# A fused attention and Fourier-mixing kernel: the third channel table's sines behind batch 0's last relu, absolute values by a sign mask, sign changes on three engines, batch 2's relay copies ahead

## Chip, cores and metric

The kernel runs on one core of one Trainium2 chip. The metric is the device time of one execution in microseconds (us); lower is better. The core has five engines with queues of their own: TensorE (PE, with its weight loads shown as PEld), VectorE (DVE), ScalarE (ACT), GpSimd (POOL) and SyncE (SP, which issues DMAs here).

## What is computed

Inputs are q, k and v of shape 8 x 12 x 448 x 64 (batch, heads, positions, head width) and two weights of 768 x 3072 and 3072 x 768, all float32.

```python
scores = q @ k.T / sqrt(64)
attn   = maximum(scores, 0) ** 2 / 448
x      = (attn @ v), heads side by side            # 8 x 448 x 768
u      = x + real(fft(fft(x, axis=positions), axis=channels))
un     = (u - mean(u)) / sqrt(var(u) + 1e-6)       # over the 768 channels
out    = u + maximum(un @ w_ch1, 0) @ w_ch2
```

## The kernel before

**Stages.** For each batch b the kernel brings q and k into transposed form (`turning`), makes scores for two heads and a quarter of the keys at a time (24 steps in a batch, line 857), takes the relu on ScalarE (line 870, PSUM to SBUF) and the square on VectorE (line 887), and multiplies by v (lines 842 and 785). After four steps one block m of 128 channels (m = 0 to 5) is complete: it is scaled and copied out of PSUM as the tile `xT` (lines 594 and 596 for batch 0, 612 later), and its two halves along the positions are added and subtracted (`fold`; `first_fold`, line 671, for batch 0).

**Mixing.** The Fourier transforms are matmuls with cosine and sine tables: `chan[0..2]` over the channels, `seq` over the positions. Blocks m = 3 to 5 use the same channel tables as m - 3, one half with its sign changed: `chan_neg[m - 3]`. For batch 0 the channel matmuls are `first_channels` (line 1307): for two row blocks i and six blocks m; two wide products for each i and m below 3, four half as wide for m from 3 on. Their sum is copied out (`pc`, line 1351), multiplied by `seq` and its negative `nseq`, normalised and transposed (`first_tail`), and only then can the first FFN matmul run (line 1793). From then on FFN matmuls of earlier tokens (lines 1793, 1821, 1848, 1933) are mixed with the attention and mixing of the later batches.

**The tables.** `build_dft` makes them on the chip. `turns` takes three VectorE operations: the product of column and row number, rounded to an integer (line 311); the difference, a fraction of a turn f (line 313); and the absolute value g as max(-f, f) (line 315). `sine` then takes two ScalarE sines from f and g (line 320). `channel_table(0)` comes first, `others()` makes tables 1 and 2. `negative()` makes `nseq` and the three `chan_neg` on VectorE (lines 357 and 361). `root_table()` (line 367) is a ScalarE square root of one column, which has the table of square roots loaded before the norm needs it.

**Transposes.** Batches 0 and 1 are transposed on TensorE (line 545), copied out on VectorE or ScalarE (line 552). From batch 2 on, VectorE copies q and k into the relay tile `qkr` (line 509), and DMAs transpose that into `qkT` (line 521). `turn_rest` starts this as one stream for batches 1 to 7.

**The order of the work.** Nothing of the order is left to the hardware's luck: a planner (`Streams.run`) draws it up when the kernel is built. Each piece of work is a stream that asks with `need(engine, us, dependencies, buffers)`. The planner always issues the request that can start earliest by its own clocks; between equals the lower rank goes first. A stream is added with two ranks, the first for TensorE, the second for all other engines:

```python
key = (ok is not None and not ok(), max(t), s[1][eng != "PE"])
```

So the estimated durations and the ranks decide the order on every engine, and a changed estimate anywhere can change the order of all that follows. On the chip, each engine then goes through its own queue strictly in that order, and waits at a semaphore where a result is not there yet. `warming` (line 2011, rank 9) fills TensorE's gaps with matmuls on zeros until batch 0's channel matmuls are done; it adds into the first of the three double banks `psS`, which then becomes the sum of the channel matmuls for i = 0. Squares have rank 0.2, copies of xT rank 0, folds of batch 0 rank 0.3, the table operations of `others` 0.15, `negative` 0.35, `turning` for batch 0 0.15, and `turn_rest` 2.

GpSimd's queue also issues the loads of q, k, v (line 413) and of the weights (lines 443 and 454); each of them waits until the load eight before it has landed.

Of the kernel before, what the change touches and what calls it, by code (L numbers as in the profile page):

```python
# [166 lines left out]
def kernel(  # L167
# [9 lines left out]
    nc = tc.nc  # L177
# [125 lines left out]
    def build_dft():  # L303
        row, col, col2 = drow, dcol, dcol2

        def turns(f, g, cols, rows, n, i):

            d = dve(n) + 0.04
            yield need("DVE", d, [indices_ready])
            r = work.tile([128, 2 * KH], mybir.dt.int32, name="dftr", tag=f"pc{TC[i][0]}", bufs=1)  # L310
            nc.vector.tensor_scalar(r[:, :n], cols, rows, None, op0=ALU.mult)
            yield need("DVE", d)
            nc.vector.scalar_tensor_tensor(f, cols, rows, r[:, :n], op0=ALU.mult, op1=ALU.subtract)
            e = yield need("DVE", d)
            nc.vector.scalar_tensor_tensor(g, f, -1.0, f, op0=ALU.mult, op1=ALU.max)
            return e

        def sine(dst, y, n, e, sign=1, bias=zero_t):
            e = yield need("ACT", act(n), [e + LATENCY["DVE"]])
            nc.scalar.activation(dst, y, AF.Sin, bias=bias, scale=sign * 2.0 * math.pi)  # L320
            dft_ready.t = e + LATENCY["ACT"]
# [13 lines left out]
        def channel_table(m):  # L335
            y = early_hid if m == 2 else work.tile([128, 4 * KH], FP32, name="dfty", tag=("u1A", "u1B")[m], bufs=1)
            e = yield from turns(y[:, 2 * KH:4 * KH], y[:, 0:2 * KH], col2, row[:, 4 + m:5 + m], 2 * KH, m % 2)
            yield from sine(chan[m][:, 0, :], y[:, 0:2 * KH], 2 * KH, e, -1, halfpi)
            yield from sine(chan[m][:, 1, :], y[:, 2 * KH:4 * KH], 2 * KH, e)
            chan_made[m].t = dft_ready.t  # L340
# [10 lines left out]

    chan_made, dft_all = [Cell() for _ in range(3)], Cell()

    def negative():

        e = yield need("DVE", 0.35, [seq_ready])
        nc.vector.tensor_scalar(nseq, seq[:, 1], -1.0, None, op0=ALU.mult)
        nseq_ready.t = e + LATENCY["DVE"]
        for m in range(3):
            e = yield need("DVE", 0.27, [chan_made[m]])  # L360
            nc.vector.tensor_scalar(chan_neg[:, m], chan[m][:, :, KH:], -1.0, None, op0=ALU.mult)
            chan_ready[m].t = e + LATENCY["DVE"]

    def root_table():

        yield need("ACT", 1.5, [dft_all, last_relu])
        nc.scalar.activation(drow[:, 7:8], zero_t, AF.Sqrt, bias=eps_t)
# [128 lines left out]

    def turning(bs):

        for b in bs:
            for g in range(NG):  # L500
                if b < 2:
# [68 lines left out]
    def fold(b, m, F, av, give, av_end):  # L570
# [58 lines left out]
        if b == 0:  # L629
# [662 lines left out]

    first_pps, first_chan = [None, None], [Cell(), Cell()]

    def first_channels(i, ms):

        n0, n1 = TC[i]
        for m in ms:
# [4 lines left out]
            for t in range(2):  # L1303
                parts = [(0, 2 * KH, chan[m][:, t, :])] if m < 3 else \
                    [(0, KH, chan[m - 3][:, t, 0:KH]), (KH, 2 * KH, chan_neg[:, m - 3, t, :])]
                for c0, c1, tab in parts:
                    nc.tensor.matmul(first_pps[i][:n1 - n0, t, c0:c1], lhsT=first_folds[m][:, t, n0:n1], rhs=tab,  # L1307
                                     start=(i == 1 and m == 0), stop=(m == MC - 1 and c1 == 2 * KH))
        if m < MC - 1:
            sch.add(first_channels(i, [MC - 1]), (0, 0))  # L1310
        else:
# [704 lines left out]
    with tc.manual_schedule():  # L2016
# [18 lines left out]
        sch.add(root_table(), (0, 0.4))  # L2035
        sch.add(negative(), (0, 0.35))
        for slot in range(6):
# [33 lines left out]
```

## Time and profile before

| what | value |
|---|---|
| median of three runs | 578.0 us (577.87 to 578.24) |
| the profiled execution | 577.99 us |
| its span in the trace | 576.0 us |
| granted TensorE clock | 1.00 |
| busy: PE, DVE, ACT, POOL | 565.0, 446.9, 336.9, 134.0 us |
| DMA, bytes moved | 81.84 MB |
| DVE, ACT busy from 17.5 to 30.4 us | 12.83 and 12.90 of 12.90 us |

Rows of the profile name the engine, the line of the kernel, the operation, and tiles as out<-in with their shapes. A busy share is an average over stages with different limits. TensorE's matmuls are pipelined, so that the lengths of neighbours overlap. Idle time is shown in square brackets with what ended it.

### The profile page before, as it was taken

How to read it: one execution, taken by the hardware profiler on the slowest of the kernel's cores; microseconds unless marked ns; L12 is line 12 of the kernel's file. 1: busy time of each engine (PE TensorE's matmuls, PEld its weight loads, DVE VectorE, ACT ScalarE, POOL GpSimd, SP SyncE). 2: the span in 40 equal slices, each digit the busy share in tenths (PEclk: the TensorE clock that was granted, in tenths of full speed). 3: DMA queues.
4: the chain of work that ended last, by engine and by line, in shares of the span. 5: the costliest groups of instructions: out<-in, count | busy, mean ns of one | idle time of the engine just before them, and what ended most of it. 6: DMA issues, size and time to landing. Idle time of an engine off the chain costs nothing.

```text
span 576.0 us, 11341 instructions
## 1 busy us (share of the span) xinstructions
PE 565.0 (98%) x4339; PEld 358.5 (62%) x4344; DVE 446.9 (78%) x1030; ACT 336.9 (59%) x538; POOL 134.0 (23%) x187
## 2 busy tenths in 40 slices
PE   8999999999999999999999999999999999999997
PEld 6466556544465546556757567568567786868864
DVE  6988775986688877997798879978978994267872
ACT  5977772977745676667559658856573160406400
POOL 8527102410134113321333116112220230000000
PEclk9999999999999999999999999999999999999999
DMA  9999999656938985799769977996654342223012
GB/s 125 206 211 249 202 219 181 174 109 78 202 78 223 175 140 119 161 167 193 140 136 197 201 126 161 177 173 113 141 107 94 109 142 85 66 73 93 2 41 97
DMA packets 133505, 81.84 MB, mean 142 GB/s; under 512 B 77516, under 2 KB 128716, under 8 KB 133452
## 3 DMA queue, kind: packets, MB, share of 16 engines
q0 software_dynamic: 40320, 33.63, 37.2%
q1 hardware_dynamic: 93132, 47.50, 36.6%
q8 instruction: 34, 0.56, 0.4%
q14 instruction: 19, 0.16, 0.1%
HBM read 62.91 MB, written 26.25 MB: 155 GB/s over the span
## 4 chain that ended last, share of the span: by engine, by line
PE 87%; DVE 9%; ACT 3%; issue 1%; DVEq 0%; ACTq 0%
PE psF L1793 31%; PE psF L1933 21%; PE psS L857 6%; PE psF L785 5%; PE psF L1821 4%; PE psS L1933 4%; PE psS L1635 3%; PE psF L1848 3%; PE psS L1332 2%; DVE sq L887 2%; ACT sq L870 1%; PE psS L785 1%; PE psS L2011 1%; PE psF L1635 1%; PE psS L932 1%; PE psS L1307 1%
## 5 line engine op out<-in xcount | busy, mean ns | idle before, releaser
L1793 PE MATMUL psF<-unT,w 128*128 128x256 bf16 (+2 forms) x1435 | 197.6, 294 | 1.3 <-ACT hT L1780 0.7
L870 ACT ACTIVATE sq<-psS 112x896 bf16<-112x896 f32 x192 | 165.2, 930 | 39.6 <-PE psS L857 39.2
L1793 PEld LDWEIGHTS <-w 128*128 128x128 bf16 x1440 | 137.5, 98 | 58.7 <-issue 12.9
L887 DVE TENSOR_TENSOR sq<-sq 112x896 bf16<-112x896 bf16 x163 | 98.4, 620 | 15.9 <-ACT sq L870 14.9
L1780 ACT ACTIVATE hT<-psF 128x512 bf16<-128x512 f32 (+3 forms) x144 | 71.7, 513 | 66.5 <-PE psF L1793 65.3
L1933 PEld LDWEIGHTS <-hT 128*128 128x128 bf16 x720 | 69.0, 98 | 50.3 <-issue 5.9
L1933 PE MATMUL psF<-w,hT 128*128 128x384 bf16 x378 | 67.1, 326 | 0.7 <-DVE xT L612 0.7
L1515 DVE TENSOR_TENSOR o<-psF,o 128x384 f32<-128x384 f32 x80 | 44.2, 553 | 25.2 <-PE psF L1933 20.8
L857 PE MATMUL psS<-qkT 64*128 64x448 bf16 (+1 forms) x384 | 52.8, 358 | 2.5 <-ACT sq L870 1.9
L413 POOL DMA_DIRECT2D vn<-in_v_dram x24 | 17.5, 730 | 105.4 <-PE psS L857 86.0
L1176 POOL TENSOR_TENSOR u<-tp,xn 112x385 f32<-112x385 f32 (+2 forms) x14 | 13.6, 974 | 109.0 <-DVE tp L1158 81.8
L857 PEld LDWEIGHTS <-qkT 64*128 64x128 bf16 (+1 forms) x384 | 17.3, 101 | 31.1 <-issue 24.1
L612 DVE TENSOR_SCALAR xT<-psF 128x224 bf16<-128x224 f32 x54 | 18.5, 383 | 21.8 <-PE psF L785 21.7
L785 PE MATMUL psF<-sq,vn 112*64 112x448 bf16 x264 | 31.3, 358 | 0.9 <-DVE hT L1778 0.9
L1204 ACT ACTIVATE un<-u,nmr,rstd 113x768 bf16<-113x768 f32 (+2 forms) x23 | 23.0, 1022 | 14.9 <-DVE nmr L1191 14.6
L413 POOL DMA_DIRECT2D qn<-in_q_dram x21 | 15.2, 724 | 62.7 <-DVE qkr L509 53.0
L1933 PE MATMUL psF<-wsum,hT 128*128 128x384 bf16 x162 | 28.8, 326 | 0.0
L1185 DVE BATCH_NORM_STATS2 stats<-u 112x6 f32<-112x384 f32 (+2 forms) x56 | 28.8, 540 | 0.0
L785 PEld LDWEIGHTS <-vn 112*64 112x64 bf16 x336 | 15.8, 109 | 19.6 <-issue 13.4
L884 ACT ACTIVATE sq<-sq 112x896 bf16<-112x896 bf16 x29 | 27.3, 950 | 0.5
L1821 PE MATMUL psF<-w,hT 128*128 128x384 bf16 x144 | 24.9, 326 | 0.0
L1848 PE MATMUL psF<-w,hT 128*128 128x384 bf16 x144 | 24.4, 326 | 0.0
(228 smaller groups left out, 783.2 us busy)
## 6 DMA issues: line engine op xcount, KB each, us to landing
out_dram<-o SPq DMA_DIRECT2D x56, 192.0 KB, 2.3
vn<-in_v_dram POOLq DMA_DIRECT2D x24, 224.0 KB, 5.0
qn<-in_q_dram POOLq DMA_DIRECT2D x21, 224.0 KB, 4.5
kn<-in_k_dram POOLq DMA_DIRECT2D x21, 224.0 KB, 7.3
w<-in_moe_w_ch_dram POOLq DMA_DIRECT2D x12, 384.0 KB, 13.2
w<-in_moe_w_ch_dram POOLq DMA_DIRECT2D x4, 1152.0 KB, 15.5
utop<-u SPq DMA_DIRECT2D x12, 336.0 KB, 3.8
o<-utop SPq DMA_DIRECT2D x16, 192.0 KB, 4.2
```

Of the source, the lines that this page charges most:

```text
L413: nc.gpsimd.dma_start(out=t, in_=src[b, hs].rearrange("h (p j) d -> p h (j d)", j=4))
L785: nc.tensor.matmul(av[h * Dh:(h + 1) * Dh, 0:S], lhsT=vn[:, c, h0 + h, :], rhs=sq[:, h, :], start=(c == 0), stop=(c == 3))
L857: nc.tensor.matmul(sc[:wide, h, 0:S].rearrange("k (c q) -> k c q", c=4), lhsT=flat[ps, k0:k0 + wide], rhs=qT[ps, m % 2], start=True, stop= ...
L870: nc.scalar.activation(r, sc[:R, :, 0:S], AF.Relu)
L887: nc.vector.tensor_tensor(r, r, r, op=ALU.mult)
L1185: nc.vector.bn_stats(stats[:n, hf, :], u[:n, hf * (D // 2):(hf + 1) * (D // 2)])
L1515: nc.vector.tensor_tensor(o, pc[:, 0:DH], o, op=ALU.add)
L1780: nc.scalar.activation(hs, ps, AF.Relu)
L1793: nc.tensor.matmul(ph[:, i * N:(i + 1) * N], lhsT=w1_sb[m][hf][:, (jj + i) * 128:(jj + i + 1) * 128], rhs=unT[:, m, 0:N], start=(m == 0), ...
L1821: nc.tensor.matmul(pc[:, 0:DH], lhsT=block(j, c), rhs=w2(j, hf), start=(j == 0), stop=(j == JC - 1))
L1848: nc.tensor.matmul(pc[:, 0:DH], lhsT=block(2 * i + k, c), rhs=weights[i], start=(start and i == 0), stop=(i == KP - 1), skip_group_check=True)
L1933: nc.tensor.matmul(pc[:, 0:DH], lhsT=lhs[i], rhs=rhs[i], start=(start and i == 0), stop=(i == KP - 1), skip_group_check=True)
```

## The change

1. In `turns` the absolute value is taken by clearing the sign bit: one VectorE operation with a constant on the 32-bit pattern. The planner's estimates for the first and third operation are lowered.
2. The two sines of channel table 2 get batch 0's last relu as a further dependency, so that they stand behind it in ScalarE's order.
3. The sign change of table 0 stays on VectorE, that of table 1 goes to GpSimd, that of table 2 to ScalarE. `root_table` also waits for the last. The rank of `negative` on these engines goes from 0.35 to 0.15.
4. The folds of batch 0 go from rank 0.3 to 0.2, level with the squares.
5. `first_channels` no longer goes through m = 0 to 4 in one stream: m = 0 comes first, then 1 to 4 are streams of their own in any order, and m = 5 follows when these are done.
6. `turn_rest` starts batch 1, then batch 2's group 0, then batch 2's groups 1 and 2 with rank 0.15 in place of 2, then batches 3 to 7.

```diff
         def turns(f, g, cols, rows, n, i):
             d = dve(n) + 0.04
-            yield need("DVE", d, [indices_ready])
+            yield need("DVE", d - 0.14, [indices_ready])
...
-            e = yield need("DVE", d)
-            nc.vector.scalar_tensor_tensor(g, f, -1.0, f, op0=ALU.mult, op1=ALU.max)
+            e = yield need("DVE", dve2(n))
+            nc.vector.tensor_scalar(g.bitcast(mybir.dt.int32), f.bitcast(mybir.dt.int32), 0x7FFFFFFF, None, op0=ALU.bitwise_and)
...
-        def sine(dst, y, n, e, sign=1, bias=zero_t):
-            e = yield need("ACT", act(n), [e + LATENCY["DVE"]])
+        def sine(dst, y, n, e, sign=1, bias=zero_t, deps=()):
+            e = yield need("ACT", act(n), [e + LATENCY["DVE"], *deps])
...
-            yield from sine(chan[m][:, 0, :], y[:, 0:2 * KH], 2 * KH, e, -1, halfpi)
-            yield from sine(chan[m][:, 1, :], y[:, 2 * KH:4 * KH], 2 * KH, e)
+            deps = [last_relu] if m == 2 else []
+            yield from sine(chan[m][:, 0, :], y[:, 0:2 * KH], 2 * KH, e, -1, halfpi, deps)
+            yield from sine(chan[m][:, 1, :], y[:, 2 * KH:4 * KH], 2 * KH, e, deps=deps)
...
         for m in range(3):
-            e = yield need("DVE", 0.27, [chan_made[m]])
-            nc.vector.tensor_scalar(chan_neg[:, m], chan[m][:, :, KH:], -1.0, None, op0=ALU.mult)
-            chan_ready[m].t = e + LATENCY["DVE"]
+            en = ("DVE", "POOL", "ACT")[m]
+            e = yield need(en, {"DVE": 0.27, "POOL": 0.7, "ACT": act(2 * KH)}[en], [chan_made[m]])
+            if en == "ACT":
+                nc.scalar.activation(chan_neg[:, m], chan[m][:, :, KH:], AF.Copy, scale=-1.0)
+                negated.t = e
+            else:
+                (nc.gpsimd if en == "POOL" else nc.vector).tensor_scalar(chan_neg[:, m], chan[m][:, :, KH:], -1.0, None,
+                                                                         op0=ALU.mult)
+            chan_ready[m].t = e + LATENCY[en]
 
     def root_table():
-        yield need("ACT", 1.5, [dft_all, last_relu])
+        yield need("ACT", 1.5, [dft_all, last_relu, negated])
...
     def turn_rest():
         yield need("SP", 0.0, [c for g in turned_at[0] for c in g])
-        sch.add(turning(range(1, B)), (2, 2))
+        sch.add(turning([1], range(NG)), (2, 2))
+        yield need("SP", 0.0, [*turned_at[1][2]])
+        sch.add(turning([2], [0]), (2, 2))
+        yield need("SP", 0.0, [*turned_at[2][0]])
+        sch.add(turning([2], [1, 2]), (2, 0.15))
+        yield need("SP", 0.0, [*turned_at[2][2]])
+        sch.add(turning(range(3, B), range(NG)), (2, 2))
...
-            sch.add(first_fold(m, x, f, gone.t + LATENCY["DVE"]), (0.3, 0.3))
+            sch.add(first_fold(m, x, f, gone.t + LATENCY["DVE"]), (0.3, 0.2))
...
     def first_channels(i, ms):
...
-        if m < MC - 1:
-            sch.add(first_channels(i, [MC - 1]), (0, 0))
+        if m == 0:
+            for x in range(1, MC - 1):
+                sch.add(first_channels(i, [x]), (5, 5))
+        elif m < MC - 1:
+            channels_made[i] += 1
+            if channels_made[i] == MC - 2:
+                sch.add(first_channels(i, [MC - 1]), (0, 0))
...
-            sch.add(first_channels(i, range(MC - 1)), (5, 5))
+            sch.add(first_channels(i, [0]), (5, 5))
...
-        sch.add(negative(), (0, 0.35))
+        sch.add(negative(), (0, 0.15))
```

More of the change, by code (lines that the diff above doesn't have):

```diff
@@ L350, in build_dft @@
         sch.add(others(), (0, 0.15))
-    chan_made, dft_all = [Cell() for _ in range(3)], Cell()
+    chan_made, dft_all, negated = [Cell() for _ in range(3)], Cell(), Cell()
     def negative():
@@ L495, with turning @@
     turned_at = [[[Cell() for _ in range(2)] for _ in range(NG)] for _ in range(B)]
-    def turning(bs):
+    def turning(bs, gs=range(NG)):
         for b in bs:
-            for g in range(NG):
+            for g in gs:
                 if b < 2:
@@ L1291, in second_turned @@
         un_left.t = group_ready[1].t = e
-    first_pps, first_chan = [None, None], [Cell(), Cell()]
+    first_pps, first_chan, channels_made = [None, None], [Cell(), Cell()], [0, 0]
     def first_channels(i, ms):
```

## The prediction

> **What bounds the kernel now.** I read the page's totals first, to see which engine could move the whole.
>
> ```profile
> span 576.0 us, 11341 instructions
> PE 565.0 (98%) x4339; PEld 358.5 (62%) x4344; DVE 446.9 (78%) x1030; ACT 336.9 (59%) x538; POOL 134.0 (23%) x187
> ```
>
> TensorE is busy 565.0 of 576.0 us, but that total counts filler matmuls (line 2011) that only keep the engine running while batch 0 is prepared. So I cut the span into stages with the busy-by-window view. Columns: window, its length, then busy us (and instructions) of PE, PE weight load, DVE, ACT, POOL, then granted clock, DMA share, GB/s.
>
> ```profile
> 8.00:17.50 9.50, 8.46 (x122) 5.43 (x120) 6.95 (x16) 8.89 (x13) 8.69 (x33) 1.00 1.36 178
> 17.50:30.40 12.90, 11.97 (x101) 5.87 (x100) 12.83 (x26) 12.90 (x20) 6.36 (x12) 1.00 1.18 210
> 30.40:37.20 6.80, 6.39 (x52) 3.98 (x50) 5.39 (x21) 4.69 (x8) 2.30 (x4) 1.00 1.08 211
> 37.20:48.30 11.10, 10.94 (x126) 8.53 (x127) 8.79 (x25) 7.57 (x18) 4.06 (x4) 1.00 1.16 224
> 48.30:64.00 15.70, 14.05 (x156) 7.79 (x155) 12.61 (x24) 12.37 (x17) 8.21 (x10) 1.00 1.19 232
> 64.00:130.00 66.00, 65.93 (x445) 36.14 (x443) 50.10 (x119) 43.55 (x65) 13.79 (x18) 1.00 0.95 173
> ```
>
> From 64 us on TensorE leaves 0.07 us unused in 66: there real FFN matmuls fill it, so work shifted on another engine is worth nothing unless a TensorE gap opens or closes. Before that, the opposite holds. From 17.5 to 30.4 us VectorE (12.83) and ScalarE (12.90) are both full, and no FFN matmul can run until batch 0 is through its attention, mixing and norm. A microsecond saved there moves the start of the FFN work, hence the end, by a microsecond. Then I read the chain in order of time over that stretch (start, length, what).
>
> ```profile
> 7.91 0.44 PE psS L2011 x6
> 8.35 0.53 PE psF L545 x16
> 8.91 0.91 ACT qkT L552
> 12.25 0.51 ACT chan L320
> 17.49 0.62 DVE qkT L552
> 20.20 0.56 DVE early L315
> 20.76 2.68 DVE sq L887 x5
> 34.41 2.79 PE psS L1307 x28
> 37.20 0.51 PE psF L545 x16
> ```
>
> From 8.91 the chain is on ScalarE, from 17.49 on VectorE (the third table's absolute value at 20.20 among the squares), and it ends in 28 channel matmuls in one block, 34.41 to 37.20. After that comes batch 0's mixing and norm, in which the diff changes nothing.
>
> **The change, part by part.** The durations of the VectorE forms in the first 37 us (groups by line with shapes apart; busy us, mean ns):
>
> ```profile
> L311 DVE TENSOR_SCALAR dftr<-dcol,drow 128x386 int32<-128x386 f32 x3 | 1.4, 477 | 0.0
> L313 DVE SCALAR_TENSOR_TENSOR dfty<-dcol,drow,dftr 128x386 f32<-128x386 f32 x2 | 1.2, 620 | 0.1
> L315 DVE SCALAR_TENSOR_TENSOR dfty<-dfty 128x386 f32<-128x386 f32 x2 | 1.1, 552 | 0.0
> L361 DVE TENSOR_SCALAR channeg<-chan 128x386 bf16<-128x386 bf16 x3 | 0.8, 290 | 0.0
> ```
>
> And the end of the stretch, in the timeline (start, length, engine, instruction):
>
> ```profile
> 32.06 1.16 ACT L870 ACTIVATE sq<-psS 112x896 bf16<-112x896 f32 x1
> 33.24 1.28 ACT L367 ACT_TABLE_LOAD   x1
> 34.53 0.29 ACT L367 ACTIVATE drow<-zero_t,eps_t 128x1 f32<-128x1 f32 x1
> 33.25 0.62 DVE L887 TENSOR_TENSOR sq<-sq 112x896 bf16<-112x896 bf16 x1
> 35.57 0.45 DVE L671 TENSOR_TENSOR fold<-xT 128x225 bf16<-128x225 bf16 x2
> 36.37 0.25 PE L1307 MATMUL psS<-chan,fold 128*128 128x193 bf16 x1
> 36.95 0.24 PE L1307 MATMUL psS<-channeg,fold 128*97 128x193 bf16 x1
> 36.90 1.05 ACT L1351 CAST pc<-psS 128x386 bf16<-128x386 f32 x2 [2.08 <-PE psS L1307]
> ```
>
> *Third table's sines behind the last relu.* Two sines at a net 0.51 us each (row at 12.25) leave the full ScalarE stretch: 1.02 us. The last relu, which now ends at 32.06 + 1.16 = 33.22, could end at 32.2. By itself this moves nothing, since VectorE is as full: it leaves VectorE alone as the limit. Behind the last relu then stand two sines (1.02) and the third sign change, taken at a sine's net 0.51 for the same 386 elements, then the table load 1.28 and the root 0.29: 32.2 + 3.1 = 35.3. The next ScalarE job, the pc copy, waits for the matmuls and stands idle 2.08 us today, so 35.3 is in time for anything later than that. The channel matmuls of m = 2 and 5 get their table at about 33.2 and 33.9, also ahead of the last fold. Cost nothing; if the relus do not come forward, 36.3 is still ahead of 36.90.
>
> A rule that speaks against this part is in the Trainium skill, "ScalarE: Activation LUTs", section "What ACT_TABLE_LOAD costs": beside a load of 1283 ns it counts a drain of about 1380 ns for every change of set. By that the queue would end at 36.7, half a microsecond behind the copy's new time and the sum below smaller by 0.5. The rows at 33.24 and 34.53 show the root starting 1.29 us after the load starts, so no drain behind the load, and the load starts 0.02 us after the last relu's end.
>
> *Absolute value by a mask.* Removed: 0.55 us each (386 elements). The new form is a one-input VectorE operation with a constant. Its nearest row is L311, 0.48 mean, which also carries a column scalar; line 313 against 315 prices that at 0.62 - 0.55 = 0.07. So 0.41, a bound of 0.55 if it is no faster, and 0.34 if the short instances count: I take 0.34, saving 0.21, because L311's mean holds one long first instance. Only the third table's is on the saturated chain; the first two lie before 17.49.
>
> *Sign changes on GpSimd and ACT.* Two times 0.25 (L361's three sum to 0.8 with one stretched) leave VectorE: 0.50. The first stays, only earlier. With the mask, VectorE's work between 17.49 and the last fold's end (35.57 + 0.45 = 36.02) drops by 0.21 + 0.50 = 0.71.
>
> *Channel matmuls one by one, folds level with squares, the first sign change ahead.* No work is added. Today the folds wait behind every square, so the matmuls pile up into the 28-block, and those of m = 5 start at 36.37 although the last fold ends at 36.02. If only these eight remain then, they start at 36.08 and end 36.37 - 36.08 = 0.29 us sooner. The price is that folds now delay squares: of VectorE's 0.71 up to all can come back as idle time if nothing is left for it between the last square and the last xT copy (33.25 + 0.62 to the fold: the values matmul and the copy lie between). Bound 0 to 0.7, taken 0, because a fold of m = 4 is still to be done there.
>
> *Start.* The second half of group 0's transposes (L545 x16) is planned only once the first half's copy has a place on VectorE, and 0.44 us of filler stands in front (row at 7.91). Two cheaper absolute values of the sequence tables let the plan place that copy sooner. Bounds 0 and 0.44; I take half, 0.2. ScalarE is full behind it, so it passes on.
>
> *GpSimd operation.* One row of GpSimd's queue there, then rows with both engines at SBUF, and one beside work from PSUM:
>
> ```profile
> 24.31 0.53 POOL L443 DMA_DIRECT2D w<-in_moe_w_ch_dram  x1 [1.33 <-DMA w<-in_moe_w_ch_dram]
> 101.00 1.26 POOL L1176 TENSOR_TENSOR u<-tp,xn 112x385 f32<-112x385 f32 x1
> 102.22 1.15 POOL L1178 TENSOR_TENSOR u<-qs,xn 112x383 f32<-112x383 f32 x1
> 101.41 1.27 DVE L1178 TENSOR_TENSOR u<-tp,xn 128x383 f32<-128x383 f32 x1
> 106.04 0.55 DVE L1178 TENSOR_TENSOR u<-tp,xn 112x383 f32<-112x383 f32 x1
> 41.55 0.98 POOL L1005 TENSOR_SCALAR un<-u,rstd,nmr 128x768 bf16<-128x768 f32 x1 [5.23 <-DVE nmr L976]
> ```
>
> GpSimd stands idle 1.33 us before a weight load, until an older load has landed; the new operation can take that place, and the loads queued behind it start later by less than its own length, with no reader of them before the FFN. Its real price is VectorE's. The VectorE addition takes 1.27 beside two GpSimd operations and 0.55 alone: 0.72 lost for 2.41 us of GpSimd, 0.3 per us. The new operation has half the elements of the one at 41.55 (0.98), so about 0.75 us: 0.22 lost. Ends 0 and 0.72. The Trainium skill, "SBUF — State Buffer", section "Who interferes with whom", says that a VectorE instruction with two SBUF inputs and a GpSimd one that reads SBUF exclude each other: whichever starts second is blocked fully. A square beside the operation would then lose up to the whole 0.75 and the sum would shrink by 0.5; the rows at 101 us agree that VectorE is held, by 0.72.
>
> *Batch 2's relay copies first.* Same four copies, earlier among VectorE's work between 95 and 113 us. What matters is what waits behind them:
>
> ```profile
> 98.29 0.43 DVE L509 COPY qkr<-kn 112x1024 bf16<-112x1024 bf16 x1 [2.19 <-DMA qkT<-qkr]
> 240.95 1.91 DVE qkr L509 x2
> 243.51 2.77 PE L1933 MATMUL psF<-w,hT 128*128 128x384 bf16 x16 [0.66 <-DVE xT L612]
> 359.78 0.95 PE L785 MATMUL psF<-sq,vn 112*64 112x448 bf16 x8 [0.93 <-DVE hT L1778]
> ```
>
> A relay copy can stand at the head of VectorE's queue until its buffer is free of the transpose before it: 2.19 us at 98.29, and the batch's mixing work queued behind it waited too. TensorE had FFN matmuls then (0.07 us unused from 64 to 130), so neither the wait nor its absence costs anything there. The rows at 240.95 and 243.51 show where it does cost: two relay copies of a later batch stand in front of an xT copy, and TensorE waits 0.66. The new streams give the whole order after 48 us a new draw. Such waits, 0.66 and 0.93, can close or open; TensorE's unused time from 48.3 to 64 is 15.70 - 14.05 = 1.65. Together 3.2 us are there to be had, and nothing in the rows limits what can open. I take a third of the 0.66, so -0.2, because one of its two causes, the relay stream, is rebuilt.
>
> **Sum.** -0.71 (VectorE's work) - 0.29 (matmul block) - 0.20 (start) + 0.22 (GpSimd beside VectorE) = -0.98 at the end of the channel matmuls, so these would end near 36.2 instead of 37.19, and -0.2 later: -1.2. The profiled execution took 577.99 (span 576.0 and 2.0 around it), the median of the runs is 578.0, so no correction between them: 576.8.
>
> **The rivals.**
> 1. *VectorE gives it back.* Mechanism: the GpSimd operation holds up a square for its whole length (0.75 instead of 0.22) and the folds drawn ahead delay the last square by up to 0.7, after which VectorE idles until the last values arrive. For it: VectorE is 12.83 of 12.90 busy, so any delay there is paid in full; the 1.27 against 0.55. Against it: from 30.40 to 37.20 VectorE is busy only 5.39 of 6.80, so folds drawn ahead mostly fill time that would be idle. Time: 577.99 - 0.98 + 0.53 + 0.6 = 578.1, and 577.3 with one of the two.
> 2. *Slower: the mixing stages open gaps.* Place: the six later mixing stages, where norm work, relay copies and hT or xT copies meet on VectorE in one order. Today two of the six leave TensorE waiting (0.66, 0.93). If the new order, shifted by a microsecond against the loads and with relay copies of its own streams, makes the other four wait 0.8 each, that is +3.2 - 1.0 = +2.2, so 580.2. It decides from the third new wait on: 2.4 - 1.0 = +1.4, over the bound. For it: the order is drawn up by a planner from estimated times, so every later stage changes, also where no code did. Against it: TensorE has 0.07 us unused in 66 up to 130 us and a stock of FFN matmuls to fill with.
> 3. *The sines' move does nothing,* since VectorE is the limit, and the folds are not drawn ahead in fact: then only 0.50 + 0.21 - 0.22 = 0.5 is left, 577.5.
>
> **How the numbers follow.** This kernel's three runs lie within 0.4 us; about 0.2% (1.16 us) is what a measurement can tell from no change, so the line lies at 576.84, just beside the forecast. The forecast's case, with its own range of 575.0 to 577.3, has 0.61: 0.46 beyond the line (the start term at its upper bound 0.44, or one TensorE wait closed) and 0.15 short of it. Rivals 1 and 3 together have 0.18, all within 0.2%. Rival 2 has 0.21. So faster 0.46, same 0.33, slower 0.21. The range runs from 574.9 (half of the 3.2 us closed as well: 577.99 - 0.98 - 1.6 = 575.4, with 0.5 for the mask and start at their best) to 579.0 (rival 2 with two to three waits); what lies above is about 0.13, below 0.06.
>
> **What would show it.** In the changed profile: the last batch 0 relu ends near 32.2 with two sines and a copy behind it ahead of the table load; the mask operation takes about 0.34; the 28-matmul block of line 1307 is down to eight or twelve; the first pc copy starts near 36 instead of 36.90, and every step of the mixing after it is earlier by the same. The forecast is wrong if the pc copy does not come forward by 0.7 or more (rivals 1 and 3: look for stretched squares beside the GpSimd operation), or if it does and the first FFN matmuls start earlier while the end does not: then waits of TensorE have opened in the mixing stages (rival 2).

## Result and profile after

| kernel | median, us | ratio to before, 95% interval |
|---|---|---|
| before | 578.1 (6 runs beside it) | |
| changed | 583.2 (581.9 to 583.6, 6 runs) | 1.008 (1.0059 to 1.0101) |

The changed kernel is slower by 0.8%, about 5 us. The profiled execution took 583.22 us, its span is 581.4. (Medians here and below are of all runs and ratios of undisturbed ones, so that a ratio need not be the quotient of the medians; three ratios further down, of "sign change on VectorE, same order", "changed, last piece behind q and k" and "room, no swap", still hold one run at a granted clock of 0.97 and are too large by it.) The totals of the page hardly differ from those before:

```profile
span 581.4 us, 11324 instructions
PE 565.4 (97%) x4330; PEld 357.6 (62%) x4330; DVE 449.0 (77%) x1033; ACT 335.7 (58%) x534; POOL 134.9 (23%) x188
```

TensorE does the same work in 5.4 us more, so it stands idle more. The busy-by-window view says where (the columns are as in the prediction):

```profile
48.30:64.00 15.70, 13.14 (x136) 6.94 (x133) 12.84 (x24) 11.81 (x17) 8.32 (x11) 1.00 1.19 228
64.00:130.00 66.00, 61.41 (x414) 34.28 (x415) 46.27 (x107) 37.37 (x56) 10.88 (x14) 0.97 1.08 162
85.00:90.00 5.00, 2.11 (x15) 0.87 (x14) 0.54 (x2) 0.98 (x2) 0.00 (x0) 1.00 1.39 91
90.00:95.00 5.00, 4.46 (x22) 2.93 (x23) 2.08 (x7) 0.98 (x2) 2.14 (x3) 0.66 1.50 188
```

From 48.3 to 130 us TensorE is unused for 2.56 + 4.59 = 7.15 us; before it was 1.65 + 0.07 = 1.72. That is 5.4 us more. (That the span grew by just as much is in part chance; the sum is drawn up further down.) From 85 to 90 us TensorE works 2.11 of 5 us, VectorE 0.54, ScalarE 0.98 and GpSimd not at all.

The part of the change that was costed in detail worked, and better than costed. ScalarE's timeline (start, length):

```profile
27.26 4.35 ACT L883 ACTIVATE sq<-psS 112x896 bf16<-112x896 f32 x5
31.51 0.61 ACT L320 ACTIVATE chan<-early,halfpi 128x386 bf16<-128x386 f32 x1
32.65 0.52 ACT L364 ACTIVATE channeg<-chan 128x386 bf16<-128x386 bf16 x1
33.19 1.28 ACT L374 ACT_TABLE_LOAD   x1
35.15 1.05 ACT L1369 CAST pc<-psS 128x386 bf16<-128x386 f32 x2 [0.37 <-PE psS L1320]
```

The last relu ends at 31.6 (33.2 before), and the first pc copy starts at 35.15 instead of 36.90: batch 0's mixing begins 1.75 us sooner. What follows undoes it. VectorE and TensorE in the timeline, and the chain of waits over the same stretch:

```profile
84.34 0.40 DVE L676 TENSOR_TENSOR fold<-fold,seqm 128x450 bf16<-128x450 bf16 x1
89.46 0.43 DVE L516 COPY qkr<-qn 112x1024 bf16<-112x1024 bf16 x1 [4.73 <-DMA qn<-in_q_dram]
89.80 0.69 DVE L625 TENSOR_SCALAR xT<-psF 128x224 bf16<-128x224 f32 x2
91.16 0.43 DVE L516 COPY qkr<-kn 112x1024 bf16<-112x1024 bf16 x1 [0.67 <-DMA kn<-in_k_dram]
```

```profile
85.96 1.15 PE L1811 MATMUL psF<-unT,w 128*128 128x384 bf16 x6
90.55 3.09 PE L1811 MATMUL psF<-unT,w 128*128 128x384 bf16 x12 [3.43 <-DVE xT L625]
93.43 0.69 PE L1350 MATMUL psS<-chan,fold 128*128 128x193 bf16 x3
103.21 0.74 PE L870 MATMUL psS<-qkT 64*128 64x448 bf16 x6 [0.67 <-DMA qkT<-qkr]
```

```profile
57.32 32.05 DMA qn<-in_q_dram
89.46 0.43 DVE qkr L516
89.89 0.61 DVE xT L625 x2
90.55 1.19 PE psF L1811 x6
...
93.24 9.92 DMA qkT<-qkr
103.21 0.74 PE psS L870 x6
```

q of batch 2's group 0, issued at 57.32, lands 32.05 us later, at 89.37. Its relay copy stands at the head of VectorE's queue and waits 4.73 us for it; the xT copy behind it is late, and TensorE waits 3.43 us for that. Then k's transpose takes 9.92 us to land, and batch 2's first scores wait for it. Before, the same copies ran without a wait:

```profile
86.08 0.42 DVE L509 COPY qkr<-qn 112x1024 bf16<-112x1024 bf16 x1
86.41 0.42 DVE L509 COPY qkr<-kn 112x1024 bf16<-112x1024 bf16 x1
```

But they were close to one: the instructions that touch kn from 55 to 60 us in the kernel before, with the time from issue to landing, show

```profile
L413 POOL DMA_DIRECT2D kn<-in_k_dram x1: 767/767/767, 56.6 to 56.6; - x1
DMA to landing us min/median/max: 29.4/29.4/29.4
```

56.6 + 29.4 = 86.0, against a copy at 86.41. Work brought forward by more than 0.4 us had to run into this load, even if it landed no later.

And the loads did land later. VectorE reached the copy of q at 84.73 in place of 86.08, 1.35 us sooner. But q itself had landed at 83.96 before (issued at 55.89, 28.07 us in flight), with 2.1 us to spare, and now landed at 89.37, 5.4 us later. So the smaller part of the 4.73 us wait is work that came forward, and the larger a load that came late. Of its lateness 1.4 us lie in the issue: GpSimd's queue had reached these loads sooner, and stood 2.90 us until an older piece of the weight had landed and 0.64 until a row store had. The rest is time in flight. Over the same stretch the DMA engines moved 182 GB/s, where it was 209 (before, then after):

```profile
64.00:90.00 26.00, 26.00 (x176) 13.82 (x174) 18.17 (x44) 17.97 (x28) 4.10 (x7) 1.00 1.26 209
64.00:90.00 26.00, 22.62 (x152) 11.58 (x151) 15.38 (x36) 16.35 (x26) 1.41 (x2) 1.00 1.36 182
```

Why they moved less is not shown by any run.

### The profile page after: what moved, and what is told of

It reads as the page before. It is cut to its first block, busy times and chain, and to the rows that moved or that the text cites. A ratio compares the mean times of both kernels' runs of the same rounds, so it can differ in the third digit from the quotient of the medians.

```text
span 581.4 us, 11324 instructions
## 1 busy us (share of the span) xinstructions
PE 565.4 (97%) x4330; PEld 357.6 (62%) x4330; DVE 449.0 (77%) x1033; ACT 335.7 (58%) x534; POOL 134.9 (23%) x188
## 4 chain that ended last, share of the span: by engine, by line
PE 78%; DMA 9%; DVE 9%; ACT 2%; issue 1%; POOL 0%; SPq 0%; DVEq 0%; POOLq 0%; ACTq 0%
PE psF L1811 27%; PE psF L1951 21%; DMA qn<-in_q_dram 6%; PE psS L870 5%; PE psS L1951 4%; PE psF L798 4%; PE psF L1839 3%; PE psS L1653 3%; PE psF L1866 3%; DMA ubot<-u,back 2%; PE psS L1350 2%; DVE sq L900 2%; DMA qkT<-qkr 2%; PE psS L798 1%; PE psF L1653 1%
```

## The experiments

**Theory L**: the computing came forward, the transfers of the first 100 us did not; VectorE's in-order queue and batch 2's first scores hit their landing. **G**: the GpSimd sign change delays the loads queued behind it. **R**: the new relay streams lose the time. **P**: the newly drawn order opens holes by itself, whatever the transfers do.

### With the order drawn anew

The first six change a request of the planner, so the order of everything later changes with them.

Relay copies of batch 2 planned 6 us later behind their loads:

```diff
-            ready[i][x].t = landed[-1] + (1.5 if g else 0.0, 3.0, 9.0, 5.0)[min(b, 3)]
+            ready[i][x].t = landed[-1] + (1.5 if g else 0.0, 3.0, 15.0, 5.0)[min(b, 3)]
```

> The changed kernel with one planner figure altered: the planner takes batch 2's loads as usable 15 us after its own estimate of their landing, in place of 9, so that their relay copies get a later place in VectorE's order. Theory L (the load of batch 2's first q lands at 89.4 us, its relay copy heads VectorE's queue for 4.7 us, the xT copy behind it is late and TensorE stands idle 3.4 us and runs at a lower clock afterwards): the wait at that relay copy falls under 1 us, TensorE's 3.4 us wait is gone, 577.0 to 579.5 us. Rival G (the GpSimd sign change, 1.6 us in front of loads in GpSimd's queue, delays every load): the same gain, since the lateness is only stepped around. Rival R (the priority of the relay copies of groups 1 and 2 is the harm): unchanged within 1 us of 583.2. Rival P (a redrawn order opens waits here and there, no single cause): within 1.5 us of 583.2, as likely above as below.

Table 1's sign change planned on VectorE:

```diff
-            en = ("DVE", "POOL", "ACT")[m]
+            en = ("DVE", "DVE", "ACT")[m]
```

> The changed kernel with the sign change of table 1 on VectorE in place of GpSimd. Rival G: the first weight load is issued near 17.4 us again (18.5 with the change), batch 2's first q lands 3 us or more earlier than 89.4, its relay copy waits under 1.5 us, at most 579.5 us. Theory L (the loads are bound by DMA throughput and compute has come forward by 1.7 us; the GpSimd operation costs the loads only the 0.4 to 1 us by which their landings differ up to 43 us): landing 0.3 to 1.5 us earlier, 581.5 to 583 us. Rival R and rival P: 583 within 1 us.

Batch 2 group 0's q and k requested ahead of the last two pieces of the second FFN weight:

```diff
+        yield from load_group(2 * NG, (0, 1))
         yield from load_w2(range(2, 4))
-        for i in range(2 * NG, B * NG):
+        yield from load_group(2 * NG, (2,))
+        for i in range(2 * NG + 1, B * NG):
```

> The changed kernel with the loads of batch 2's first q and k issued ahead of the last two pieces of the second weight, each of which is five times as large. Theory L: they land before 75 us, no relay copy waits for a load, TensorE's 3.4 us wait at 87 us is gone and the 1.7 us gained by 37 us reaches the end: 575.5 to 578 us, unless the second weight, now later by about 3 us, is waited for. Rival G: the same. Rival R: unchanged within 1 us of 583.2. Rival P: anything from 577 to 584 with waits at other places.

The kernel before, with table 1's sign change on GpSimd and nothing else:

```diff
-            e = yield need("DVE", 0.27, [chan_made[m]])
+            en = ("DVE", "POOL", "DVE")[m]
+            e = yield need(en, {"DVE": 0.27, "POOL": 0.7}[en], [chan_made[m]])
...
+            (nc.gpsimd if en == "POOL" else nc.vector).tensor_scalar(chan_neg[:, m], chan[m][:, :, KH:], -1.0, None,
+                                                                     op0=ALU.mult)
```

> The kernel before with one part of the change alone: the sign change of table 1 on GpSimd (0.7 us in the planner's account, 1.6 us long in the changed kernel's trace). In the kernel before, k of batch 2's first group lands at 86.0 us and its relay copy starts at 86.4. Rival G: the loads behind it land 2 us or more later, the relay copy waits, 580.5 us or more. Theory L: landings later by at most 1 us, 577.5 to 579.5 us. Rivals R and P: within 1 us of 578.

The changed kernel without its relay part:

```diff
-        sch.add(turning([1], range(NG)), (2, 2))
...
+        sch.add(turning(range(1, B), range(NG)), (2, 2))
```

> The changed kernel with the relay steps added as in the kernel before, in one row (2, 2) for all groups, and the rest of the change kept; the order is drawn anew. Theory R (the part that puts batch 2's groups 1 and 2 ahead makes the loss): 577 to 579. Theory L: group 0's copies have the same rank in both, the work ahead of them is as early, so the copy waits for q as before: a wait of 3 to 5 us and 582 to 584, up to 2 us of either sign from the new order.

The kernel before with that part alone (the same lines the other way):

> The kernel before with the part on batch 2's relay copies alone; the order is drawn anew. Theory R: 580.5 to 583. Theory L: the mixing starts where it did and the copies of group 0 come after their load: 577.3 to 579.3.

| run | median, us | ratio to before (95%) |
|---|---|---|
| copies later | 580.3 | 1.0041 (1.0024 to 1.0059) |
| sign change on VectorE | 592.0 | 1.0237 (1.0206 to 1.0269) |
| q and k requested early | 586.6 | 1.0155 (1.0112 to 1.0198) |
| before, sign change on GpSimd | 579.2 | 1.0018 (0.9995 to 1.0041) |
| changed, old relay | 589.6 | 1.0195 (1.0169 to 1.0221) |
| before, relay part | 578.2 | 1.0002 (0.9977 to 1.0027) |

Copies later and sign change on VectorE, each from 64 to 130 and from 130 to 245 us:

```profile
64.00:130.00 66.00, 64.70 (x437) 35.58 (x437) 50.43 (x114) 40.15 (x60) 11.21 (x14) 1.00 1.06 174
130.00:245.00 115.00, 111.92 (x719) 57.89 (x718) 91.78 (x206) 73.90 (x127) 34.92 (x39) 1.00 0.80 144
```

```profile
64.00:130.00 66.00, 65.73 (x441) 36.36 (x441) 50.69 (x114) 37.44 (x57) 11.48 (x14) 1.00 1.04 167
130.00:245.00 115.00, 105.62 (x662) 53.28 (x659) 81.60 (x182) 68.55 (x116) 24.84 (x30) 0.96 0.78 130
```

In both the hole from 64 to 130 is mostly or wholly gone. In the first that is as L says: the copy of q runs later, at 91.86, behind its load. The second speaks for G as much, since q landed at 84.75 there, 4.6 us sooner than in the changed kernel, where L had allowed 1.5. Both times were missed, by L and by G alike: the first run leaves TensorE 3.1 us unused from 130 to 245 and the second 9.4, where the changed kernel leaves none. So a redrawn order can cost more than the effect under test, and such runs can't size it. They still settle one point. R falls: the relay part costs nothing in the kernel before (at most 0.3% by the interval), and the changed kernel without it is worse and keeps its hole, with TensorE busy 60.95 of the 66 us from 64 to 130. In that run, too, the times that R and L gave were missed, since its new order left TensorE 4.6 us unused from 130 to 245 and 3.5 from 245 to 360. Moving the loads up as requests gave 586.6, also a miss: there the relay copies ran at 74.4, but a later one waited 6.75 us for the transpose before it.

### With every engine's order kept

From here on the planner sees the same requests, so that each engine but GpSimd goes through the same list as in the parent kernel. First, the sign change carried out by VectorE at its old place in the list:

```diff
-                (nc.gpsimd if en == "POOL" else nc.vector).tensor_scalar(chan_neg[:, m], chan[m][:, :, KH:], -1.0, None,
-                                                                         op0=ALU.mult)
+                nc.vector.tensor_scalar(chan_neg[:, m], chan[m][:, :, KH:], -1.0, None, op0=ALU.mult)
```

> The changed kernel with every engine's order as planned, except that the sign change of table 1 is carried out by VectorE at the same place in the order instead of GpSimd. Theory G: the first weight load is issued 1 to 1.2 us earlier, q of batch 2 lands 2 to 5 us earlier, the copy's wait falls from 4.73 to under 1.5, the time is 579 to 580.5. Theory L: the loads' end is set by the bytes ahead of them, q lands at most 1.2 us earlier, the wait falls to 3.5 to 4.7, VectorE's added 0.27 us costs 0 to 0.3 in the mixing, the time is 582 to 583.4.

Twelve matmuls to no purpose ahead of batch 0's mixing, in the changed kernel and in the one before:

```diff
+            for _ in range(12 if t == 0 and hf == 0 else 0):
+                nc.tensor.matmul(pu[:, 0:D // 2], lhsT=warm[:, 0:128], rhs=warm[:, 0:D // 2], start=True, stop=True)
```

> The changed kernel with every engine's order as planned, and twelve matmuls of 128x384 to no purpose (about 2 us) ahead of batch 0's first mixing rows. Theory L: the hole at the relay copy shrinks by as much as the work is put back, so that the time stays within 0.7 us of the changed kernel's (582.5 to 583.9) and the copy's wait falls to about 2.7. Theory P: nothing of it is hidden, 585 to 585.5.

> The kernel before with the same twelve matmuls ahead of batch 0's first mixing rows. Theory L: here the copies wait for no load at all, so nothing hides the added time: 579.8 to 580.4, with no wait of a relay copy on q. Theory P: the same here. If 578.0 to 578.6 comes out, the mixing start isn't on the path at all in either kernel, and a gain there was never worth anything.

| run | median, us | ratio to before (95%) |
|---|---|---|
| sign change on VectorE, same order | 582.5 | 1.0117 (1.0052 to 1.0182) |
| changed, 2 us of delay | 582.3 | 1.0077 (1.0059 to 1.0095) |
| before, 2 us of delay | 579.7 | 1.0036 (1.0018 to 1.0053) |

The two delays are the plainest evidence that in the changed kernel the transfers set the time. Two microseconds of empty work cost the kernel before 1.6 us, and the changed kernel nothing. In the latter the copy's wait shrank and the first scores came up against the transposes (VectorE, then TensorE):

```profile
86.03 0.43 DVE L516 COPY qkr<-qn 112x1024 bf16<-112x1024 bf16 x1 [0.95 <-DMA qn<-in_q_dram]
```

```profile
100.25 1.11 PE L870 MATMUL psS<-qkT 64*128 64x448 bf16 x6 [2.65 <-DMA qkT<-qkr]
```

G falls as the main cause, by the time: without the GpSimd operation and with the same order 582.5 us remain, where G gave 579 to 580.5. The copy of q still waited 2.62 us there, and the first scores 2.31 us for the transposes. Whether the operation makes the loads land later stays open. Without it the copy of q ran at 86.35, 3 us ahead of the changed kernel's 89.46, and in the kernel before with it q landed at 86.06 in place of 83.96, both as G has it. But with it the copy also ran at 86.03, in the delayed kernel, with the same order of loads. So the landing varies by 3 us for another reason too; which one was not settled.

Now the transfers. The last piece of the second FFN weight behind batch 2 group 0's q and k in GpSimd's queue, and in another kernel not loaded at all, so that the matmuls read the third piece in its place and that kernel leaves out a quarter of the weight:

```diff
+            if i == 3:
+                put_off.append(load)
+            else:
+                load()
...
+            if i == 2 * NG and x == 1:
+                put_off.pop()()
```

> The changed kernel with every engine's order as planned; only in GpSimd's queue of transfers the last of the four pieces of the second FFN weight (1152 KB) is issued behind batch 2 group 0's q and k instead of ahead of them. Theory L (the work came forward, the loads did not, and the relay copy at the head of VectorE's queue waits for q): q lands some 5 to 7 us earlier (82 to 84), the copy's 4.73 us wait and TensorE's 3.43 us hole go, 64 to 130 shows 64 to 65.5 us of TensorE work in place of 61.41, and the time is 577 to 579.5. Theory P (the new order of the whole kernel opens holes everywhere and the relay wait is one of many): at most 1.5 us come back, 581.7 or more. Theory G (the GpSimd operation alone delays the loads): the same gain as L at the copy, so it isn't told apart here.

```diff
-            t = wpool.tile([128, 6, D], BF16, name=f"w2_{i}")
+            t = w2_sb[2] if i == 3 else wpool.tile([128, 6, D], BF16, name=f"w2_{i}")
+            if i < 3:
```

> The changed kernel with every engine's order as planned; the last of the four pieces of the second FFN weight isn't loaded (1152 KB off the queue), its place in the matmuls is taken by the third piece, so the FFN's result is not the reference's. Theory L (the transfers of the first 100 us, not the engines, set when batch 2's first scores can run): q of batch 2 lands 5 to 7 us earlier, its relay copies wait for nothing, the two transposes land by 96, TensorE has no hole of over 1 us between 64 and 130, and the time falls to 575.8 to 578.0, at or below the kernel before. Theory P (the new order itself, whatever the transfers do): the holes stay, 581.5 to 583.5.

> The kernel before without the same piece's load (the same part of the FFN is not the reference's). Theory L: there no relay copy waits for a load and TensorE has no hole between 64 and 130, so that nothing is to be had: 577.4 to 578.3. Under P the same. If it falls by 1 us or more, the kernel before is bound by its transfers too.

| run | median, us | ratio to before (95%) |
|---|---|---|
| changed, last piece behind q and k | 584.6 | 1.0132 (1.0076 to 1.0189) |
| changed, last piece not loaded | 577.0 | 0.9976 (0.9966 to 0.9987) |
| before, last piece not loaded | 578.4 | 0.9994 (0.9969 to 1.0019) |

Putting the piece behind only moved the wait: the copy ran at 83.78 without waiting, and TensorE waited for the transposes, now in flight beside that piece:

```profile
101.76 1.30 PE L881 MATMUL psS<-qkT 64*128 64x448 bf16 x6 [5.36 <-DMA qkT<-qkr]
```

L's 577 to 579.5 was missed here, since it had counted the first wait only. With 1152 KB gone from the queue both waits go, and 6.2 us come back, as L said (575.8 to 578.0); windows of that kernel:

```profile
64.00:90.00 26.00, 25.66 (x179) 14.10 (x179) 17.30 (x42) 17.24 (x28) 2.81 (x4) 1.00 1.38 183
90.00:100.00 10.00, 10.00 (x69) 6.10 (x68) 6.78 (x12) 4.51 (x6) 4.87 (x5) 1.00 0.85 123
100.00:130.00 30.00, 29.95 (x201) 15.89 (x201) 26.57 (x66) 19.87 (x28) 3.60 (x5) 1.00 0.67 147
```

The same removal gives the kernel before nothing (0.9969 to 1.0019). P falls as the whole cause: with the same order on every engine the holes are gone. And the two runs without the piece are the nearest there is to the change's price where transfers don't bind: 578.4 to 577.0, a gain of 1.4 us in the medians, near the 1.2 that was forecast. Their two intervals overlap, so a smaller gain, or none, is not excluded.

Can the whole kernel have that? Seven loads of batch 2 that nothing reads before 106 us were put behind the row stores at 98 us, with the weight's last piece behind q and k as above; then without that swap, on the kernel before (there five loads only: group 1's q and k stay in place, since their copies come earlier in its order), and with the sign change on VectorE:

```diff
+            if b == 2 and (g > 0 or x == 2):
+                later[0 if g + (x == 2) == 1 else 1].append(load)
+            else:
+                load()
...
+        if b == 1 and bot is ubot[1]:
+            for load in later[ch][1 - ch:] + later[ch][:1 - ch]:
+                load()
```

> The changed kernel, whole and with the order of TensorE, VectorE, ACT and SyncE as planned; only GpSimd's queue of transfers is put in another order: batch 2 group 0's q and k ahead of the last piece of the second FFN weight, and the seven loads of batch 2 that nothing reads before 106 us (group 0's v, groups 1 and 2) behind the row stores of the stage at about 98 us. Theory L (the transfers of the first 100 us set batch 2's first scores): q lands at 79 to 80 and its relay copies wait for nothing, the two transposes land by 96, no hole of over 1 us on TensorE between 64 and 115, 576.0 to 578.0, below the kernel before. If the weight's last piece alone, in flight beside the transposes, delays them as much as the whole queue did, 579 to 582. Theory P: 582 to 584.

> The same with the last piece of the weight left ahead of q and k: q lands as late as in the changed kernel (87 to 89), the copy's wait of 3 to 5 us stays, but the transposes find the DMA engines free and land 4 to 6 us after their issue instead of 10. Theory L: 580 to 582. If the transposes' landing is all that counts and the copy's wait is nothing, 577 to 578.5.

> The kernel before with q and k of batch 2 group 0 ahead of the weight's last piece and five loads (group 0's v, group 2) behind the row stores; group 1's q and k stay where they were, since their copies come earlier in this order. Theory L: no gain, since nothing waits for a load there: 577.5 to 578.6, up to 580 if the transposes now meet the weight's piece.

> The first of these with the sign change of table 1 back on VectorE at the same place. Theory G would have it gain another 1 us (loads 1.2 us earlier); theory L, with the loads out of the way, nothing of it, and VectorE's 0.27 us more ahead of batch 0's squares: 0 to 0.4 us above the first.

Finally group 1's q and k back at their old place (`g == 2` for `g > 0`), and the weight's piece behind those too:

> The first of the four with group 1's q and k left where they were (they landed too late there: a copy waited 1.70 us for k at 106 and TensorE 1.16 us behind it); group 0's v and four other loads stay behind the row stores. Theory L: no hole of over 1 us between 64 and 130, 576.6 to 577.6, below the kernel before by 0.1 to 0.25%. If group 1's q and k, in flight until about 91, delay the two transposes past 97, 577.6 to 579.

> The same with the weight's last piece behind group 1's q and k too: the same bytes ahead of the transposes, the weight's piece lands about 3 us later (92) and is first used at about 95 to 98: 576.6 to 577.8, or, if TensorE comes to wait for the weight, 578 to 580.

| run | median, us | ratio to before (95%) |
|---|---|---|
| room | 578.6 | 1.0008 (0.9988 to 1.0028) |
| room, no swap | 582.5 | 1.0079 (1.0042 to 1.0115) |
| before, room | 585.3 | 1.0109 (1.0047 to 1.0171) |
| room, sign change on VectorE | 578.8 | 1.0002 (0.9980 to 1.0024) |
| room, group 1's q and k kept | 578.7 | 1.0012 (0.9998 to 1.0026) |
| the same, weight's piece last | 578.3 | 1.0009 (0.9997 to 1.0022) |

The first of them: the copy of q, the first scores, and two windows.

```profile
84.16 0.42 DVE L535 COPY qkr<-qn 112x1024 bf16<-112x1024 bf16 x1
```

```profile
96.71 0.74 PE L889 MATMUL psS<-qkT 64*128 64x448 bf16 x6
```

```profile
64.00:90.00 26.00, 26.00 (x184) 14.44 (x184) 16.96 (x42) 17.23 (x27) 0.00 (x0) 1.00 1.29 186
100.00:130.00 30.00, 28.41 (x189) 14.94 (x188) 24.91 (x62) 19.29 (x27) 7.58 (x11) 1.00 1.20 196
```

So an order of transfers alone, with nothing left out, takes back 4.6 of the 5 us. It needs both parts: without the swap the copy of q again waits 3.06 us and 582.5 remains. The GpSimd operation makes no difference (578.6 and 578.8). What is left, 1.59 us from 100 to 130, stood in that trace as the same wait again: a copy of group 1 waits 1.70 us for its k. Keeping those two loads early changed little (578.7 and 578.3). None of these versions beats the kernel before, and L's times for them (576 to 578, then 576.6 to 577.6 and to 577.8) were missed by 0.5 to 1.1 us.

The control missed. On the kernel before, putting off the loads cost 7 us, not 0 to 2. In its trace TensorE waits 4.9 us in two waits for ScalarE's norm output, the longer of them 4.7:

```profile
PE psS L1127 <- ACT un L1223: 4.9, 2, 4.7
```

ScalarE was late because VectorE was, and VectorE stood at a relay copy again, now for group 2's q, one of the loads put off:

```profile
115.98 0.43 DVE L528 COPY qkr<-qn 112x1024 bf16<-112x1024 bf16 x1 [7.17 <-DMA qn<-in_q_dram]
```

So the control doesn't show what the steps cost without a late load; it shows the same mechanism made in the other kernel.

## Why the prediction was wrong

**The first part held, and was undersized.** The end of the channel matmuls was to come at -0.98; it and the pc copy came at -1.75. The start (0.20) came as taken: the sixteen transposes that began at 8.28 begin at 8.08. The mis-sized term is VectorE's work between 17.49 and the last fold's end, 0.71. The busy-by-window view of that stretch, before (the fold ends at 36.02) and after (at 34.33):

```profile
17.49:36.02 18.53, 17.20 (x136) 8.80 (x135) 18.23 (x46) 17.31 (x26) 8.36 (x15) 1.00 1.15 210
17.49:34.33 16.84, 16.10 (x133) 7.66 (x132) 16.05 (x42) 16.76 (x23) 8.29 (x17) 1.00 1.15 205
```

VectorE's work there fell by 2.18 us, from 18.23 to 16.05. Its idle time grew by 0.49, from 0.30 to 0.79, which the prediction had taken as 0 with a bound of 0.7. So the last fold ends 1.69 sooner. The matmuls behind it gave almost nothing of their 0.29. Most of the 2.18 us are the two sign changes (0.50, as taken) and the third table's three operations. In the kernel before, VectorE's timeline has them in the full stretch (0.41 + 0.62 + 0.56 = 1.59 us):

```profile
19.10 0.41 DVE L311 TENSOR_SCALAR dftr<-dcol,drow 128x386 int32<-128x386 f32 x1
19.55 0.62 DVE L313 SCALAR_TENSOR_TENSOR early<-dcol,drow,dftr 128x386 f32<-128x386 f32 x1
20.20 0.56 DVE L315 SCALAR_TENSOR_TENSOR early<-early 128x386 f32<-128x386 f32 x1
```

In the changed one they lie 7.4 us sooner, where VectorE stood idle:

```profile
11.66 0.42 DVE L311 TENSOR_SCALAR dftr<-dcol,drow 128x386 int32<-128x386 f32 x1
12.11 0.62 DVE L313 SCALAR_TENSOR_TENSOR early<-dcol,drow,dftr 128x386 f32<-128x386 f32 x1
12.77 0.55 DVE L315 TENSOR_SCALAR early<-early 128x386 int32<-128x386 int32 x1
```

The prediction credited this table with 0.21 for a cheaper mask, and the mask, at 0.55 against 0.56, wasn't cheaper there (beside the GpSimd operation, of which more below). What counted was that the order drew all three operations ahead. No run takes this term apart; it is read from the traces.

**The GpSimd operation** took 1.60 us, not 0.75. VectorE paid little, about the 0.22 that was taken: the mask beside it took 0.55, and in the kernel with the sign change on VectorE and the same order 0.36, so 0.19. Rival 1, and the lock between the two engines that the prediction took from the Trainium skill ("SBUF — State Buffer", "Who interferes with whom"), would have it cost VectorE 0.75. The mask in that kernel's timeline, and the GpSimd operation in the changed kernel's groups by line (busy us, mean ns):

```profile
13.11 0.36 DVE L315 TENSOR_SCALAR early<-early 128x386 int32<-128x386 int32 x1
```

```profile
L367 POOL TENSOR_SCALAR channeg<-chan 128x386 bf16<-128x386 bf16 x1 | 1.6, 1604 | 0.4 <-ACT chan L320 0.4
```

By that rule whoever starts second is blocked. VectorE's two-input operation had started first, at 12.11, ahead of GpSimd's at 12.19, and it took 0.62 us, as it does without GpSimd beside it (0.60), which agrees. How long the GpSimd operation takes with nothing beside it no run shows; in the kernel before, at 35.2 us, it took 1.36.

**The step that failed** is in "Batch 2's relay copies first". It found a relay copy's wait of 2.19 us, and concluded that "neither the wait nor its absence costs anything there", because TensorE had FFN matmuls from 64 to 130. That holds while the work behind VectorE's queue head is not due. At 84 us it was due at once, and the wait cost TensorE 3.43 us. The prediction had the mechanism in rival 2, "shifted by a microsecond against the loads and with relay copies of its own streams", but put it in the later mixing stages, gave it +2.2 us and a chance of 0.21, and took the full windows before as evidence that nothing could open between 64 and 130. A full window says that nothing waits now; it doesn't say by how much. The margin here was 0.4 us for k and 2.1 for q. The landings themselves were a term at nothing: the prediction saw "no reader of them before the FFN" behind GpSimd's new operation, but batch 2's q and k stand in that queue too, their reader is the relay copy, and q landed 5.4 us later.

**What it cost** adds up about so. Lead at the mixing: 1.75. Added idle time of TensorE, 48 to 130 us: 5.4. And the clock: after the 3.43 us hole the granted clock was 0.66 from 90 to 95, and three channel matmuls took 0.69 us instead of 0.41; 5.00 x 0.34 = 1.7 us. So -1.75 + 5.4 + 1.7 = +5.4, the difference of the spans (TensorE's idle time elsewhere moved by some tenths, so the match is closer than this method can promise). The first 1.75 doesn't show as less idle time, since it took away filler matmuls, 92 short ones in place of 106. The Trainium skill, "TensorE: Matmul & The Clock Gate", "Part 1: The HAM clock gate", says that TensorE falls to half its clock after an idle window of about 3.4 us and stays there for as long again. By that an estimate for the row is (5.0 - 3.4 x 0.5) / 5.0 = 0.66, and it reads 0.66.

**The order made it worse.** The changed order would reach batch 2's first scores at 96.7 (the room run), the kernel before reached them at 100.3. The transposes allowed 103.2, in the delayed kernel 100.3. So even where the changed kernel got its scores at the old time it ended 4.2 us later (582.3 less 578.1): its busy time leaves 0.83 + 2.39 = 3.2 us unused from 64 to 100, where the kernel before has none. Fewer matmuls stood ahead of the scores in TensorE's list. Of the FFN matmuls of line 1821 (1839 in the changed kernel) 48 run ahead of them in the kernel before and 30 in the changed one, and eighteen such matmuls take 3.09 us. The new order had moved this cover behind the scores, so P holds for a part: the order opened no hole by itself, but it left less to fill one.

## What to carry to other kernels

Before crediting work that comes forward, follow each load that the next stage reads: issue plus time to landing against the reader's start. Where they differ by less than the gain, the gain ends there, and an in-order queue turns it into a loss, because what stands behind the waiting head waits too. Leave room for the landing to move as well: the same load landed at 83.96, 85.9, 86.3 and 89.4 us in four of these kernels. And an order drawn up from estimates has to be re-drawn with the transfers' measured times, or held fixed while one thing is tested.

## What was not expected of the hardware

The transposes that SyncE issues take longer beside many loads that GpSimd issues: k's took 9.92 us from issue to landing in the changed kernel, while in the kernel before the pair took

```profile
DMA to landing us min/median/max: 6.3/6.6/7.0
```

The Trainium skill, "DMA: Bandwidth & Descriptors", "Issuing engines are not separate DMA queues", says that transfers of all issuing engines run on the same 16 DMA engines and interleave; the run that let the copy go early beside the weight's last piece agrees, with a wait of 5.36 us for the transposes. And the same order of loads landed q of batch 2 at 89.4 in one kernel and by 86.0 in another, with 2 us of matmuls as the only difference in the program.
